# Planning the main expert slots with priority and ahead of the dual slots, turning their list in the second early slot's layer 2, and stacking the token tiles over v

## The chip, the cores and the metric

The kernel runs on one core of one Trainium2 chip. The metric is the device time of one execution in microseconds (us), and the number to compare with is the median of three runs: 804.94 us (804.16 to 805.5). TensorE (PE, with its weight loads as PEld) multiplies matrices, VectorE (DVE) and ScalarE (ACT) do elementwise work, GpSimd (POOL) issues the indirect transfers, and SyncE (SP) issues the plain ones. [...]

## The reference

Linear attention feeds a mixture of experts with one expert per token. All data are float32.

```python
# attention: 8 batches, 8 heads, 576 positions, head size 64, 128 features
proj = x @ w_phi                       # for q and for k
proj = proj - max(abs(proj))           # over the features
phi  = concat(exp(proj), exp(-proj))   # 256 features
kv, z = phi(k).T @ v, phi(k).sum(positions)
x = (phi(q) @ kv) / (phi(q) @ z + 1e-6)          # [8, 576, 512] over all heads

# experts: 8 of them, 512 -> 1024 -> 512
logits = x @ w_gate;  local = sigmoid(x @ w_local)
e[s] = argmax(logits[s]) if s == 0 or local[s] < 0.5 else e[s-1]
out[s] = softmax(logits[s])[e[s]] * (relu(x[s] @ w1[e[s]]) @ w2[e[s]])
```

There are 4,608 tokens. How many go to which expert is known only when the kernel runs.

## The kernel before, in words

**Attention** (`step` and what it calls) runs over pairs of chunks of 128 positions. `proj` multiplies k and q by `w_phi` and makes the tiles `sb` and `kp`; `qtr` turns the q part into `qp` (pool `feat`, eight buffers); `kv` adds up `kvp` from `kp` and `v`; `num` multiplies `qp` with the finished `kvs` into the PSUM tile `nm` (line 312), from which `end` (lines 329 to 340) writes the normalised rows `xo` to DRAM and keeps the gate logits `lg`. `kq` and `v` are loaded ahead into pool `front2`; `m`, `sb`, `kp` lie in `front3`.

**Gating** (`gate`) runs once for each of four batch pairs. It finds each token's expert and its place in the expert's list, and nine indirect writes on POOL (line 555) scatter token number and probability into the DRAM table `lst`. For the last pair the PE steps of this work are set between the matmuls of the first early slot, through the hooks in `soon`.

**Early slots.** Half way through attention `plan_early` picks three groups of 256 tokens (each a "slot" with two units of 128 tokens of one expert), for which the first batch pairs already give enough tokens. `slots(self.eslots)` computes these three after attention. A slot is: `tokens` (PE turns gathered rows `xg` at line 905; ACT and DVE split them into the high part `xhi` and the low part `xlo`, lines 914 and 915), `layer1` (four steps `f2` of 24 matmuls into one of two PSUM buffers `l1`; each gives `hh` on ACT, line 954, and `hl` on DVE, line 955), and `layer2` (for each unit `k` 24 matmuls into `l2`, then `y` on DVE, line 1006, and an indirect write of the rows, line 1009). Every product is three matmuls (lines 919 to 921). The weights come in eight pieces per slot: SP loads a piece into `wraw` (line 842), ACT rounds it to `whi` (line 852), DVE makes `wlo` (line 853).

**Main slots.** `plan_main` counts the tokens of all experts (`units_so_far`), subtracts what the early slots took, and hands out the rest to slots of four, two and one unit ("m" in the names of its tiles), and the rests of at most 64 tokens to dual slots, in which two experts share a tile ("h0", "h1"). It is a generator in two parts. The first part is all the planning on DVE, tiny operations on 36 by 8 numbers, and the three indirect reads of the lists from `lst` into the tile `lr` in `fetch` (line 616: the main list by `p_rim`, the duals' lists by two `p_rih`). The second part turns `lr` on PE (line 629) and copies it to `tok` and `prob`, with which the rows `xg` of the main slots are gathered. Before the change DVE plans the duals first and the main slots after them, and POOL reads the lists in the order of the program and of the planner below. SP reads the expert numbers of the main slots (`value_load`, line 829) before it can load their weights.

**Where the two parts stand.** `later` is a list of functions that the first early slot's `layer2` calls after `f` 0 and 2 of each unit; its third, after `f` 0 of unit 1, is the first part. `asides={1: more}` runs the second part between layer 1 and layer 2 of the second early slot. `final` calls the generator once more in the third early slot, when it has already ended.

**Order and memory.** Except for the PE order of attention, the order on each engine is made by a planner that walks the program with its own costs: of what is ready it takes what stands first in the program. `tc.high_priority()` moves the instructions inside it ahead of all others that are ready; `issue_after` keeps a PE instruction behind a given one. Pools are laid out as two stacks. On the right stack `open_main` puts its pools where attention's right pools were: `front2` at the end of the memory (20,088 bytes per partition: four `kq` of 3,072, then five `v` of 1,560), then `front3` (about 28,770), then `feat` (eight `qp` of 4,096). A new tile waits until the readers of every old tile that it overlaps are done. Before the change the weight pool `moe_wr` (32,768 bytes: four `whi`, four `wlo`) comes first and the token pool `moe_x2` (16,384 bytes: two `xhi`, two `xlo`) after it, so that `moe_x2` reaches from 32,768 to 49,152 bytes from the end, and its first `xhi` overlaps the last `qp` buffer by about 300 bytes. On the left stack `open_rest` puts the pool `moe_l1`, with three more `wraw` buffers, where the pool with `lr` was; the first main weight load goes there and so has to wait until `lr` is turned.

Of the kernel before, what the change touches and what calls it, by code (L numbers as in the profile page):

```python
# [9 lines left out]
I32 = mybir.dt.int32  # L10
AF = mybir.ActivationFunctionType
ALU = mybir.AluOpType
AX = mybir.AxisListType
# [4 lines left out]
DM, E, FF = 512, 8, 1024  # L18
# [4 lines left out]
NU_E = NT // 128  # L23
# [7 lines left out]
WE, WR, WL = 8, 4, 1  # L31
# [13 lines left out]
HALFWAY, EARLY, QUADS, PAIRS, SINGS, GUARD, DUALS, GUARD_D = 2, 3, 3, 7, 10, 6, 4, 2  # L45
# [4 lines left out]
class Kernel:  # L50
# [9 lines left out]
    def run(self):  # L60
        nc, tc, A = self.nc, self.tc, self.A
        act, dve = self.act, self.dve
        with ExitStack() as root:
            self.const = self.mkpool(root, "const", 1, "left")
            dram = self.mkpool(root, "dram", 1, "left", DRAM)
            self.xs = dram.tile([NT + 1, DM], F32, name="xs")


            self.lst = dram.tile([E * NT + 128, PLACE], F32, name="lst")
            first = self.const.tile([128, 256], F32, name="first")  # L70
            self.sp.dma_start(first[:, 128:256], A["first"][:, 384:512])
            self.ident, self.w2 = first[:, 0:128], first[:, 128:256]
            self.cnt = self.const.tile([128, E], BF16, name="cnt")
            dve.memset(self.cnt, 0.0)

            warm = self.const.tile([128, E], BF16, name="warm")
            act.activation(warm, self.cnt, AF.Exp)

            self.wgi = self.const.tile([128, NHP, 2, 9], F32, name="wgi")
            self.pool.memset(self.wgi, 0.0)  # L80

            self.vs = [[self.const.tile([128, 2, D + 1], F32, name=f"vs{k}{b}") for b in (0, 1)] for k in (0, 1)]
            for x in self.vs:
                for t in x:
                    self.pool.memset(t, 0.0)

            self.moe_early = self.mkpool(root, "moe_e", WE, "left")
            self.mxg = self.mkpool(root, "moe_xg", 2, "left")
            back, front = ExitStack(), ExitStack()
            self.back2 = self.mkpool(back, "back2", 2, "left")  # L90
            self.small = self.mkpool(back, "small", 1, "left")

            self.pr = self.small.tile([128, 2, NC, PLACE], F32, name="pr")
            self.pool.memset(self.pr, 0.0)
            self.pskv = self.mkpool(back, "pskv", 1, "left", PSUM)
            self.psb = self.mkpool(back, "psb", 2, "left", PSUM)


            self.front2 = self.mkpool(front, "front2", 2, "right")
            self.front3 = self.mkpool(front, "front3", 3, "right")  # L100
            self.feat = self.mkpool(front, "feat", 8, "right")
            self.psf = self.mkpool(front, "psf", 2, "right", PSUM)
            self.wphases = [(self.moe_early, WE)]

            self.scattering = False
            self.tail, self.eslots, self.scattered = False, [], []
            self.g, self.ch, self.kvb, self.lg = {}, {}, {}, {}
            n = NBP * NHP * NC
            self.todo, self.turns, self.gates, self.background = [], [], [], []
            self.fetched = 0  # L110
            for gi in range(3):
                self.fetch_kqv(gi)
                if gi == 0:
                    self.sp.dma_start(first[:, 0:128], A["first"][:, 256:384])
                    self.consts()
            with tc.manual_schedule(engines={mybir.EngineType.PE}):
                for p in range(n // 2):
                    while self.fetched < n // 3 and self.fetched * 3 < 2 * p + 8:
                        self.fetch_kqv(self.fetched)
                    if FILL <= p < FILL + 4:  # L120
                        self.fill(p - FILL)
                    self.step(p, n)
            self.tail = True
            p = n // 2
            while p < n // 2 + KVLAG + 1 or self.todo or self.turns or self.gates:
                self.step(p, n)
                p += 1
            for x in self.background:
                for _ in x:
                    pass  # L130
            front.close()
            self.open_main(root)
            plan = self.plan_main()
            more = lambda: next(plan, None)
            go = self.advance

            def rest():
                for _ in self.last_gate:
                    pass
            no = lambda: None  # L140
            self.slots(self.eslots, {1: more}, more, soon=[no, self.fetched_last, go, no, go, no, go, rest],
                       later=[no, no, more])
            back.close()
            self.open_rest(root)
            self.moe()
# [452 lines left out]
    def fetch(self, es, k, n, name, wait, halves=()):  # L598
# [8 lines left out]
        while self.scattering:  # L607
            yield STEP
        full = n
        n += DUALS if halves else 0  # L610
        lr = self.small.tile([NU + DUALS, 128 * PLACE], F32, name="lr")[0:n]
        parts = [(lr[0:full], 128, ri[0:full, :])]
        w = 64 * PLACE
# [96 lines left out]
    def plan_main(self):  # L710
        dve = self.dve
# [1 line left out]
        u1, u = self.units_so_far(127, 7, "m1"), self.units_so_far(63, 7, "m")  # L713
        r0 = self.psm([NU, E], "r0", I32)
        dve.tensor_sub(r0, u, self.taken)
        hf = self.psm([NU, E], "hf")
        dve.tensor_sub(hf, u1, u)
        full = self.floats(u, "full")
        ih = self.prefix(hf, "ih")

        q = self.psm([NU, 2], "q")
        dve.tensor_scalar(q[:, 0:1], self.slote[:, 0:1], 4.0, None, ALU.mult)
        dve.scalar_tensor_tensor(q[:, 0:1], self.slote[:, 1:2], 2.0, q[:, 0:1], ALU.mult, ALU.add)
        dve.tensor_scalar_add(q[:, 1:2], q[:, 0:1], 1.0)
        eh, rh = [], []
        for z in (0, 1):
            name = f"h{z}"
            es, _ = self.find(ih, hf, q[:, z:z + 1], name)
            oh = self.psm([NU, E], "oh" + name)
            dve.tensor_scalar(oh, self.iota8[0:NU, :], es, None, ALU.is_equal)  # L730
            dve.tensor_mul(oh, oh, full)
            k = self.psm([NU, 1], "k" + name)
            dve.tensor_reduce(k, oh, AX.X, ALU.add)
            dve.scalar_tensor_tensor(k, es, float(NU_E), k, ALU.mult, ALU.add)
            ri = self.psm([NU, 1], "ri" + name, I32)
            dve.tensor_scalar_mul(ri, k, 2.0)
            rh.append(ri)
            eh.append(self.experts(es, name))

        def level(r, shift, cap, name):  # L740
            fi = self.psm([NU, E], "fi" + name, I32)
# [11 lines left out]
        f1 = self.floats(r2, "f1")  # L753
        i1 = self.prefix(f1, "i1")

        over = self.psm([1, 2], "over")
        dve.tensor_scalar(over[:, 0:1], i1[0:1, E - 1:E], float(GUARD - SINGS), 0.0, ALU.add, ALU.max)
        dve.tensor_scalar(over[:, 1:2], ih[0:1, E - 1:E], float(2 * (GUARD_D - DUALS)), 0.0, ALU.add, ALU.max)
        self.more = self.psm([1, 1], "more", I32)
        dve.tensor_copy(self.more, over[:, 0:1])  # L760
        self.over = self.psm([1, 1], "overi", I32)
        dve.tensor_add(self.over, over[:, 0:1], over[:, 1:2])

        def mix(a, b, c, name):
            t = self.psm([NU, E], name)
            dve.tensor_scalar(t, a, mq, None, ALU.mult)
# [8 lines left out]
        dve.scalar_tensor_tensor(bef, p4, mps, self.taken, ALU.mult, ALU.add)  # L775
        dve.scalar_tensor_tensor(bef, p2, ms, bef, ALU.mult, ALU.add)
        es, j = self.find(incl, cnt, cq, "m")
        oh = self.psm([NU, E], "ohm")
        dve.tensor_scalar(oh, self.iota8[0:NU, :], es, None, ALU.is_equal)
        dve.tensor_mul(oh, oh, bef)  # L780
# [1 line left out]
        dve.tensor_reduce(k, oh, AX.X, ALU.add)  # L782
        dve.tensor_add(k, k, half)
        dve.scalar_tensor_tensor(k, j, size, k, ALU.mult, ALU.add)
        ei = self.experts(es, "m")
        f = self.fetch(es, k, NU, "m", 1, rh)
        next(f)
        yield
        try:
# [12 lines left out]


    def open_main(self, root):
        self.w_right = self.mkpool(root, "moe_wr", WR, "right")

        self.mxt = self.mkpool(root, "moe_x2", 2, "right")
        self.mx2 = self.mkpool(root, "moe_h2", 2, "right")
        self.psm4 = self.mkpool(root, "moe_ps1", 1, "right", PSUM)
        self.psl = self.mkpool(root, "moe_ps2", 2, "right", PSUM)  # L810
        self.wphases = [(self.moe_early, WE), (self.w_right, WR)]
# [203 lines left out]
            else:  # L1015
                held.append(put)

    def slots(self, order, asides={}, final=None, held=None, soon=(), later=()):
        first = order[0]
        for g in range(len(first["n"])):  # L1020
            for f in self.tokens(first, g):
# [3 lines left out]
        for i, s in enumerate(order):  # L1025
# [3 lines left out]
            last = len(s["n"]) - 1  # L1029
            for gi in range(last):  # L1030
                self.layer1(s, gi, [])
            between = self.tokens(new, 0, bool(soon) and i == 0) if new else [lambda: None, final] if final else []
            rest = self.layer1(s, last, between, () if i else soon)
            if soon and i == 0:
                rest = later
            if i in asides:
                asides[i]()
            for f in between:
                f()
            for gi in range(last + 1):  # L1040
# [140 lines left out]
```

## Time and profile before

| what | value |
|---|---|
| median of three runs | 804.94 us (804.16 to 805.5) |
| the profiled execution's own time | 804.99 us |
| its span, first to last instruction | 803.1 us |
| PE busy | 770.4 us (96%) |
| DVE busy | 513.1 us (64%) |
| ACT busy | 401.0 us (50%) |
| POOL busy | 157.3 us (20%) |
| attention's last matmul (line 312) ends | about 320.4 us |
| early slots on PE | about 321.6 to 404 us |
| main and dual slots | from there to the end |

The span and the time differ by 1.9 us, which lie before the first and after the last instruction. Of the views, "waits" adds up for one engine who it waited for; "timeline" lists instructions in order of time, with the idle time before them and its releaser in square brackets; "windows" gives, for a stretch of time, the busy time and the number of instructions of each engine, the granted clock of TensorE and the share and rate of the transfers; "lines" gives groups of instructions with busy time and mean duration. A q behind an engine's name is its sequencer, which waits and issues transfers.

### The profile page before, as it was taken

How to read it: one execution, taken by the hardware profiler on the slowest of the kernel's cores; microseconds unless marked ns; L12 is line 12 of the kernel's file. 1: busy time of each engine (PE TensorE's matmuls, PEld its weight loads, DVE VectorE, ACT ScalarE, POOL GpSimd, SP SyncE). 2: the span in 40 equal slices, each digit the busy share in tenths (PEclk: the TensorE clock that was granted, in tenths of full speed). 3: DMA queues.
4: the chain of work that ended last, by engine and by line, in shares of the span. 5: the costliest groups of instructions: out<-in, count | busy, mean ns of one | idle time of the engine just before them, and what ended most of it. 6: DMA issues, size and time to landing. Idle time of an engine off the chain costs nothing.

```text
span 803.1 us, 23175 instructions
## 1 busy us (share of the span) xinstructions
PE 770.4 (96%) x9674; PEld 678.4 (84%) x9674; DVE 513.1 (64%) x939; ACT 401.0 (50%) x708; POOL 157.3 (20%) x165
## 2 busy tenths in 40 slices
PE   6899999999998998999899999999999999999993
PEld 5899989998897888888798997698998998589983
DVE  5677798789878886785653224543866823768631
ACT  4666666666687565333542123532744713657410
POOL 0000001200275231064231202201421311111100
PEclk9999999999999999999999999999999999999997
DMA  6754545454576723455932775832966769959300
GB/s 198 220 152 127 134 133 143 129 140 126 176 227 208 232 71 96 145 170 178 362 124 93 271 268 206 294 101 94 350 219 202 272 229 411 356 193 320 124 27 14
DMA packets 77227, 151.29 MB, mean 188 GB/s; under 512 B 8524, under 2 KB 50828, under 8 KB 77078
## 3 DMA queue, kind: packets, MB, share of 16 engines
q1 hardware_dynamic: 67424, 127.33, 49.6%
q0 software_dynamic: 7424, 20.08, 7.0%
q10 hardware_dynamic: 2272, 2.37, 0.9%
q8 instruction: 77, 1.26, 0.6%
q14 instruction: 30, 0.25, 0.1%
HBM read 128.21 MB, written 22.06 MB: 187 GB/s over the span
## 4 chain that ended last, share of the span: by engine, by line
PE 83%; DVE 7%; DMA 4%; issue 2%; ACT 2%; SPq 1%; another core or an unknown queue 0%; POOLq 0%; DVEq 0%; POOL 0%; ACTq 0%
PE l L919 15%; PE l L921 15%; PE l L920 15%; PE kvp L253 8%; PE pj L211 8%; PE nm L312 8%; PE qt L231 4%; PE l L932 4%; DMA wraw<-in_w2h 2%; PE tr L905 2%; DVE m L214 1%; DVE sb L216 1%; PE nm L291 1%; DMA kq<-in_kqT 1%; DMA wraw<-in_w1h 1%
## 5 line engine op out<-in xcount | busy, mean ns | idle before, releaser
L852 ACT CAST whi<-wraw 128x1024 fp32r<-128x1024 f32 x136 | 142.2, 1048 | 165.3 <-PE l L921 67.2
L853 DVE TENSOR_TENSOR wlo<-wraw,whi 128x1024 fp32r<-128x1024 f32 x128 | 156.3, 1223 | 71.0 <-ACT whi L852 69.6
L919 PE MATMUL l<-xhi,whi 128*128 128x256 f32 x512 | 147.1, 288 | 1.4 <-ACT xhi L914 1.3
L920 PE MATMUL l<-xlo,whi 128*128 128x256 f32 x512 | 144.8, 283 | 1.3 <-DVE xlo L915 1.3
L921 PE MATMUL l<-xhi,wlo 128*128 128x256 f32 x512 | 144.7, 283 | 0.0
L919 PE MATMUL l<-whi,hh 128*128 128x512 f32 x288 | 114.8, 399 | 1.6 <-ACT hh L954 1.6
L214 DVE TENSOR_REDUCE m<-pj 128x8 f32<-128x1024 f32 x72 | 87.8, 1219 | 44.5 <-PE pj L211 44.1
L921 PE MATMUL l<-whi,hl 128*128 128x512 f32 x288 | 113.9, 396 | 1.4 <-DVE hl L955 1.4
L920 PE MATMUL l<-wlo,hh 128*128 128x512 f32 x288 | 113.1, 393 | 0.0
L234 ACT ACTIVATE qp<-qt 128x512 f32<-128x512 f32 x144 | 84.6, 604 | 53.6 <-PE qt L231 53.2
L220 ACT ACTIVATE kp<-sb 128x512 f32<-128x512 f32 x144 | 82.8, 622 | 51.2 <-DVE sb L216 43.5
L919 PEld LDWEIGHTS l<-xhi,whi 128*128 128x128 f32 x512 | 97.6, 191 | 4.3 <-issue 2.2
L920 PEld LDWEIGHTS l<-xlo,whi 128*128 128x128 f32 x512 | 97.7, 191 | 1.9 <-DVE xlo L915 1.5
L921 PEld LDWEIGHTS l<-xhi,wlo 128*128 128x128 f32 x512 | 97.8, 191 | 0.1
L211 PE MATMUL pj<-first,kq 64*128 64x128 f32 x1152 | 86.1, 291 | 6.7 <-DMA kq<-in_kqT 6.7
L216 DVE TENSOR_TENSOR sb<-pj,m 128x1024 f32<-128x1024 f32 x72 | 88.1, 1224 | 4.1
L312 PE MATMUL nm<-kvs,qp 128*64 128x74 f32 x2304 | 86.3, 228 | 1.5 <-ACT kvs L293 1.5
L1009 POOL DMA_INDIRECT out<-y,p_tokm x31 | 39.1, 1263 | 244.4 <-DVE y L1006 243.8
L211 PEld LDWEIGHTS pj<-first,kq 64*128 64x128 f32 x1152 | 72.2, 193 | 12.3 <-issue 5.0
L312 PEld LDWEIGHTS nm<-kvs,qp 128*64 128x64 f32 x2304 | 79.1, 136 | 2.2 <-ACT kvs L293 2.0
L253 PE MATMUL kvp<-v,kp 128*64 128x65 f32 x2048 | 76.2, 224 | 0.0
L955 DVE SCALAR_TENSOR_TENSOR hl<-l,hh 128x512 fp32r<-128x512 f32 x64 | 43.9, 686 | 43.5 <-ACT hh L954 43.5
(229 smaller groups left out, 1053.3 us busy)
## 6 DMA issues: line engine op xcount, KB each, us to landing
wraw<-in_w1h SPq DMA_DIRECT2D x68, 512.0 KB, 5.7
wraw<-in_w2h SPq DMA_DIRECT2D x68, 512.0 KB, 4.8
kq<-in_kqT SPq DMA_DIRECT2D x47, 384.0 KB, 3.9
v<-in_va SPq DMA_DIRECT2D x48, 195.0 KB, 3.7
xs<-xo SPq DMA_DIRECT2D x48, 128.0 KB, 2.1
whi<-in_w1h SPq DMA_DIRECT2D x8, 512.0 KB
wlo<-in_w1h SPq DMA_DIRECT2D x8, 512.0 KB, 5.5
whi<-in_w2h SPq DMA_DIRECT2D x8, 512.0 KB
```

What stands on the lines that cost most here:

```text
L211: self.last_pe = self.pe.matmul(t[:, h, i % 2, j, :], kq[r, j, s], self.w2[r], start=True, stop=True)
L214: dve.tensor_reduce(m, f, AX.X, ALU.max, apply_absolute_value=True)
L216: self.last_dve = dve.tensor_sub(sb.rearrange("p h c j f -> p (h c j) f"), f, m.unsqueeze(2).broadcast_to([128, 8, 128]))
L220: self.last_act = act.activation(kp[:, :, :, sg, :].rearrange("p c h f -> p h c f"), sb[:, :, :, 0], AF.Exp, scale=1.0 - 2 * sg)
L234: self.act.activation(qp[:, sg], t, AF.Exp, scale=1.0 - 2 * sg)
L253: self.pe.matmul(self.kvp[r, sg, h], self.ch[i]["kp"][:, h, sg, r], self.v(i, b)[:, h], start=first and n < 2, stop=last and n >= 6)
L312: self.pe.matmul(e["t"][r, c - c0, h, :], self.ch[i]["qp"][:, sg, h, q0 + r.start:q0 + r.stop], kvs[:, sg, h, :], start=sg == 0, stop=sg == 1)
L852: self.act.copy(hi, raw)
L853: (low or self.dve).tensor_sub(lo, raw, hi.bitcast(F32))
L919: mm(o, ah, bh, start=first, stop=False)
L920: mm(o, ah, bl, start=False, stop=False)
L921: self.last_pe = mm(o, al, bh, start=False, stop=last)
```

## The change

Four things change.

1. `open_main` opens the token pool `moe_x2` before the weight pool `moe_wr`. The token tiles then take the last 16,384 bytes, over the `kq` and `v` buffers, and the weight tiles 16,384 to 49,152 bytes from the end; now the first `whi` buffer overlaps the last `qp` by about 300 bytes.
2. `more` runs each part of `plan_main` inside `tc.high_priority()`.
3. In `plan_main` the planning of the duals and of the two overflow counts becomes a function `duals`, which `fetch` calls after the main list's row numbers `p_rim` are made. The main slots' operations come first in the program, and their expert numbers `ei` directly after `find`.
4. The second part of `plan_main`, with the turning of `lr`, moves from between the layers of the second early slot into its layer 2, after `f` 0 of unit 1. `asides` and `final` go, and `later` becomes a list for each slot.

No instruction of the computation is added or removed.

```diff
             plan = self.plan_main()
-            more = lambda: next(plan, None)
+            def more():
+                with tc.high_priority():
+                    next(plan, None)
...
-            self.slots(self.eslots, {1: more}, more, soon=[no, self.fetched_last, go, no, go, no, go, rest],
-                       later=[no, no, more])
+            self.slots(self.eslots, soon=[no, self.fetched_last, go, no, go, no, go, rest], later=[[no, no, more]] * 2)
...
         full = n
-        n += DUALS if halves else 0
+        if halves:
+            n, halves = n + DUALS, halves()
...
     def plan_main(self):
...
         dve.tensor_sub(r0, u, self.taken)
-        hf = self.psm([NU, E], "hf")
-        dve.tensor_sub(hf, u1, u)
-        full = self.floats(u, "full")
-        ih = self.prefix(hf, "ih")
...
         es, j = self.find(incl, cnt, cq, "m")
+        ei = self.experts(es, "m")
...
         dve.scalar_tensor_tensor(k, j, size, k, ALU.mult, ALU.add)
-        ei = self.experts(es, "m")
-        f = self.fetch(es, k, NU, "m", 1, rh)
+        hf = self.psm([NU, E], "hf")
+        eh = []
+
+        def duals():
+            dve.tensor_sub(hf, u1, u)
+            full = self.floats(u, "full")
+            ih = self.prefix(hf, "ih")
...
+            return rh
+
+        f = self.fetch(es, k, NU, "m", 1, duals)
...
     def open_main(self, root):
+        self.mxt = self.mkpool(root, "moe_x2", 2, "right")
         self.w_right = self.mkpool(root, "moe_wr", WR, "right")
-        self.mxt = self.mkpool(root, "moe_x2", 2, "right")
...
-            between = self.tokens(new, 0, bool(soon) and i == 0) if new else [lambda: None, final] if final else []
+            between = self.tokens(new, 0, bool(soon) and i == 0) if new else []
             rest = self.layer1(s, last, between, () if i else soon)
-            if soon and i == 0:
-                rest = later
-            if i in asides:
-                asides[i]()
+            if i < len(later):
+                rest = list(later[i])
```

More of the change, by code (lines that the diff above doesn't have):

```diff
@@ L715, in plan_main @@
         dve.tensor_sub(r0, u, self.taken)
-        hf = self.psm([NU, E], "hf")
-        dve.tensor_sub(hf, u1, u)
-        full = self.floats(u, "full")
-        ih = self.prefix(hf, "ih")
[L721 to L738, printed above, removed]
         def level(r, shift, cap, name):
@@ L754, in plan_main @@
         i1 = self.prefix(f1, "i1")
[L756 to L762, printed above, removed]
         def mix(a, b, c, name):
@@ L784, in plan_main @@
         dve.scalar_tensor_tensor(k, j, size, k, ALU.mult, ALU.add)
-        ei = self.experts(es, "m")
-        f = self.fetch(es, k, NU, "m", 1, rh)
+        hf = self.psm([NU, E], "hf")
[4 more added lines that the diff above has]
+            ih = self.prefix(hf, "ih")
+            q = self.psm([NU, 2], "q")
+            dve.tensor_scalar(q[:, 0:1], self.slote[:, 0:1], 4.0, None, ALU.mult)
+            dve.scalar_tensor_tensor(q[:, 0:1], self.slote[:, 1:2], 2.0, q[:, 0:1], ALU.mult, ALU.add)
+            dve.tensor_scalar_add(q[:, 1:2], q[:, 0:1], 1.0)
+            rh = []
+            for z in (0, 1):
+                name = f"h{z}"
+                es, _ = self.find(ih, hf, q[:, z:z + 1], name)
+                oh = self.psm([NU, E], "oh" + name)
+                dve.tensor_scalar(oh, self.iota8[0:NU, :], es, None, ALU.is_equal)
+                dve.tensor_mul(oh, oh, full)
+                k = self.psm([NU, 1], "k" + name)
+                dve.tensor_reduce(k, oh, AX.X, ALU.add)
+                dve.scalar_tensor_tensor(k, es, float(NU_E), k, ALU.mult, ALU.add)
+                ri = self.psm([NU, 1], "ri" + name, I32)
+                dve.tensor_scalar_mul(ri, k, 2.0)
+                rh.append(ri)
+                eh.append(self.experts(es, name))
+            over = self.psm([1, 2], "over")
+            dve.tensor_scalar(over[:, 0:1], i1[0:1, E - 1:E], float(GUARD - SINGS), 0.0, ALU.add, ALU.max)
+            dve.tensor_scalar(over[:, 1:2], ih[0:1, E - 1:E], float(2 * (GUARD_D - DUALS)), 0.0, ALU.add, ALU.max)
+            self.more = self.psm([1, 1], "more", I32)
+            dve.tensor_copy(self.more, over[:, 0:1])
+            self.over = self.psm([1, 1], "overi", I32)
+            dve.tensor_add(self.over, over[:, 0:1], over[:, 1:2])
+            return rh
+        f = self.fetch(es, k, NU, "m", 1, duals)
         next(f)
@@ L1016, in layer2, with slots @@
                 held.append(put)
-    def slots(self, order, asides={}, final=None, held=None, soon=(), later=()):
+    def slots(self, order, held=None, soon=(), later=()):
         first = order[0]
```

## The prediction

> **What bounds the kernel now.** I read the page first, then who PE waits for, then the order of time on PE, ACT and SP around those waits, and last the stretches with their granted clock. The page's span and first section:
>
> ```profile
> span 803.1 us, 23175 instructions
> ...
> PE 770.4 (96%) x9674; PEld 678.4 (84%) x9674; DVE 513.1 (64%) x939; ACT 401.0 (50%) x708; POOL 157.3 (20%) x165
> ```
>
> PE sets the end, so only its idle time and its slow clock can be won. The windows view (columns: length; busy time and count of PE, PEld, DVE, ACT, POOL; clock; transfer share; GB/s) shows where these lie near the change:
>
> ```profile
> 320.36:327.24 6.88, 4.34 (x22) 4.16 (x23) 4.42 (x20) 1.34 (x3) 0.00 (x0) 0.75 0.50 158
> 391.17:398.92 7.75, 5.51 (x20) 4.05 (x20) 6.23 (x7) 5.09 (x6) 0.48 (x1) 0.78 1.02 398
> 405.00:780.00 375.00, 374.99 (x2451) 325.54 (x2450) 197.98 (x225) 158.09 (x223) 66.82 (x56) 1.00 0.63 220
> ...
> 356.00:370.50 14.50, 13.59 (x86) 11.38 (x86) 11.71 (x37) 7.10 (x9) 4.53 (x4) 1.00 0.54 177
> ```
>
> In the main slots (405 to 780 us) PE idles 0.01 us, so what is won or lost before them passes whole to the end. There are two holes. The first, where the early slots begin, has 6.88 - 4.34 = 2.54 us of idle time, and its clock of 0.75 costs 6.88 x 0.25 = 1.72 us more: 4.26 us. The second, in the third early slot, has 7.75 - 5.51 = 2.24 us idle and 7.75 x 0.22 = 1.70 us of clock: 3.94 us. Next come 14.50 - 13.59 = 0.91 us of small waits in the second early slot.
>
> **The first hole** in order of time (PE and ACT):
>
> ```profile
> 312.25 2.24 PE L312 MATMUL nm<-kvs,qp 128*64 128x74 f32 x62
> 314.43 1.09 PE L905 MATMUL tr<-first,xg 128*128 128x128 f32 x8
> ...
> 317.57 2.79 PE L312 MATMUL nm<-kvs,qp 128*64 128x74 f32 x80 [0.29 <-ACT kvs L293]
> 321.63 0.47 PE L919 MATMUL l<-xhi,whi 128*128 128x256 f32 x2 [1.27 <-ACT xhi L914]
> 323.38 0.38 PE L920 MATMUL l<-xlo,whi 128*128 128x256 f32 x1 [1.27 <-DVE xlo L915]
> ...
> 313.07 2.95 ACT L852 CAST whi<-wraw 128x1024 fp32r<-128x1024 f32 x3
> 320.46 1.07 ACT L914 CAST xhi<-tr 128x512 fp32r<-128x512 f32 x2 [2.94 <-PE nm L312]
> ```
>
> The first slot's tokens are turned by 314.43 + 1.09 = 315.52, but ACT writes `xhi` at 320.46 and names the last `nm` matmul (317.57 + 2.79 = 320.36) as its releaser. That matmul doesn't make the data; it is the last reader of the old `qp` buffer under `xhi`. PE then has nothing until `xhi`, and again until `xlo`.
>
> *What the stacking does to it.* After the change `xhi` lies over `kq` and `xlo` over the end of `kq` and `v`. The last reader of `v`, the `kvp` matmuls, is done before the 62 `nm` matmuls that begin at 312.25. So both casts can follow the turning at 315.5; ACT sits idle for 2.94 us of the time up to 320.46. Two `xhi` take 1.07 us; two `xlo` on DVE (0.68 us each, below) then end about 318.7 to 320 between the `xo` work. PE goes from the last `nm` straight into layer 1, idle time 2.54 us won. The stretch of half clock came right behind this idle time, and I take it to go with it: 1.72 us. Term: -4.26 us, with ends 0 and -4.26.
>
> [...]
>
> *What it costs.* The first right-hand `whi` buffer now lies over the last `qp`, so one of the three casts at 313.07 moves behind 320.36. It changes places with the two `xhi` (one cast of 2.95/3 = 0.98 us against 1.07 us on ACT; one `wlo` of 1.22 against two `xlo` of 1.37 on DVE). Its data are for the second early slot. One `wraw` of three stays taken some 6 us longer. I take 0, hidden by ACT's idle time; without that cover the cast stands ahead of an `hh` and costs its 0.98.
>
> **The second hole.** PE's waits between 310 and 400 us, and ACT's order there:
>
> ```profile
> PE l L919 <- ACT hh L954: 1.6, 2, 1.1
> PE l L921 <- DVE hl L955: 1.4, 3, 0.6
> ...
> 382.79 0.59 ACT L954 ACTIVATE hh<-l 128x512 fp32r<-128x512 f32 x1
> ...
> 388.74 1.05 ACT L852 CAST whi<-wraw 128x1024 fp32r<-128x1024 f32 x1 [3.08 <-DMA wraw<-in_w2h]
> 389.70 0.59 ACT L954 ACTIVATE hh<-l 128x512 fp32r<-128x512 f32 x1
> 391.11 1.05 ACT L852 CAST whi<-wraw 128x1024 fp32r<-128x1024 f32 x1 [0.82 <-DMA wraw<-in_w2h]
> 392.39 1.05 ACT L852 CAST whi<-wraw 128x1024 fp32r<-128x1024 f32 x1 [0.24 <-DMA wraw<-in_w2h]
> 393.35 0.59 ACT L954 ACTIVATE hh<-l 128x512 fp32r<-128x512 f32 x1
> 393.84 1.04 ACT L852 CAST whi<-wraw 128x1024 fp32r<-128x1024 f32 x1
> ```
>
> PE waits for `hh` and `hl` of the third slot, and these stand in ACT's list behind casts of the first main slot's weights, which wait for transfers that run at a share of 1.02. Why do those transfers come so late? SP's waits from 361 to 378 us, its reads of the expert numbers, its loads; PE's turning of the list; POOL's reads of the list and their landing:
>
> ```profile
> SPq L842 <- DMA lr<-lst,p_rim: 3.2, 1, 3.2
> ...
> SPq L842 <- PE pt L629: 0.5, 1, 0.5
> ...
> L829 SPq TENSOR_LOAD <-p_eim x14: 266/274/562, 362.2 to 369.9; - x14
> ...
> 374.57 2.06 SPq L842 DMA_DIRECT2D wraw<-in_w1h  x4
> ...
> 371.87 0.39 PE L921 MATMUL l<-whi,hl 128*128 128x512 f32 x1
> 374.02 0.41 PE L629 MATMUL pt<-first,lr 40*128 40x40 f32 x2
> ...
> 359.03 0.91 POOL L616 DMA_INDIRECT lr<-lst,p_rih  x1 [3.21 <-DVE p_f L646]
> 360.25 1.66 POOL L616 DMA_INDIRECT lr<-lst,p_rih  x1 [0.30 <-DVE p_lem L586]
> 368.92 0.92 POOL L616 DMA_INDIRECT lr<-lst,p_rim  x1 [5.67 <-DVE p_rim L605]
> DMA to landing us min/median/max: 2.8/4.3/5.1
> ```
>
> SP spends 8 us (362.2 to about 370.2) on 14 expert numbers, then 3.7 us on `lr`: the main list is read last, at 368.92, because DVE plans it last.
>
> *Moved planning, reads and turning.* With the main chain first and all of it urgent, the three reads follow each other from about 359.0 at a pitch of 1.2 us; the last goes out near 361.5 and lands at most 5.1 us later, 366.6. The expert numbers come sooner too, so SP's 8 us fall among the third slot's loads, where they push weights that layer 2 wants only after the `hh` above; hidden, and 0. What holds `lr` now is its new place on PE. After `f` 0 of unit 1 means after the matmul at 371.87, so at about 372.1 instead of 374.02: 1.9 us earlier on PE's own clock. The whole of it shifts with the first term, and the landing at 366.6 is still ahead of 372.1 - 4.3 = 367.8; were the reads later than that, the 1.9 would shrink. The main `xg` reads on POOL come 1.9 us earlier with `tok`.
>
> *What 1.9 us earlier loads bring.* ACT's order is written out beforehand. Now two casts stand between the third and the fourth `hh`. The planner places casts by its own transfer times; with loads 1.9 us earlier it has room for one more cast ahead of each `hh`. The third `hh` then follows the cast of 391.11 instead of 388.74: 391.11 + 1.05 - 1.9 = 390.26, later than 389.70. The fourth follows the cast of 393.84: 393.84 + 1.04 - 1.9 = 392.98, earlier than 393.35 by 0.37. The last wait decides: -0.37, the clock still falls. If the order stays as it is, the term is -1.9 and the clock's -1.70, -3.60. I take -0.37, because the same planner that set casts ahead of `hh` before has the same cause to do it again.
>
> *DVE's burst of planning.* DVE rows of 346.2 to 368.7 us, and the first `hl` of the second slot:
>
> ```profile
> 346.20:368.70 22.50, 21.80 (x142) 19.10 (x141) 20.85 (x89) 12.28 (x15) 11.40 (x10) 1.00 0.56 168
> ...
> L853 DVE TENSOR_TENSOR wlo<-wraw,whi 128x1024 fp32r<-128x1024 f32 x9 | 11.0, 1219 | 0.6 <-ACT whi L852 0.5
> L955 DVE SCALAR_TENSOR_TENSOR hl<-l,hh 128x512 fp32r<-128x512 f32 x4 | 2.7, 674 | 0.0
> L915 DVE TENSOR_TENSOR xlo<-tr,xhi 128x512 fp32r<-128x512 f32 x2 | 1.4, 684 | 1.0 <-ACT xhi L914 1.0
> L1006 DVE TENSOR_SCALAR y<-l,p_probe 128x512 f32<-128x512 f32 x1 | 0.7, 732 | 0.0
> ...
> 346.20:356.10 9.90, 4.87 (x4) 0.00 (x0) 1.00 0.48 126
> 356.08 0.67 DVE L955 SCALAR_TENSOR_TENSOR hl<-l,hh 128x512 fp32r<-128x512 f32 x1
> ```
>
> Planning is 20.85 - 11.0 - 2.7 - 1.4 - 0.7 = 5.05 us of DVE. Ahead of `hl` at 356.08 stand four `wlo` (4.87) and one `y` (0.73), so up to 9.9 - 4.87 - 0.73 = 4.3 of it is there already. Made urgent, at most 0.75 us more gets ahead of `hl` and of `y`, which PE awaits; against that, the 0.91 us of small waits behind it can shrink as the planning is gone. Ends +0.75 and -0.91; I take 0, between them. The swap of main and dual planning has the same operations.
>
> **Sum** against the execution's own 804.99 us (median of the runs 804.94, so no correction): 804.99 - 4.26 - 0.37 = 800.36 us.
>
> **Rivals.**
>
> *Both holes close* (0.23): ACT's order stays and the loads' 1.9 us count whole. For it: 1.9 of 2.24 us idle would do. Against it: the same lists are planned anew. 804.99 - 4.26 - 3.60 = 797.13.
>
> *The gap closes, the slow clock stays* (0.07): The half clock comes from something that stays, such as the short waits among the `nm` matmuls before 320 us. 804.99 - 2.54 - 0.37 = 802.08. Against it stands that in both holes half clock follows idle time at once. [...]
>
> *The change doesn't open the start* (0.14): `xhi` is written late for another reason, such as the `wlo` and `xo` work on DVE holding `xlo` beyond the last `nm`, so that PE waits as long. For it: `xlo` has its own 1.27 us wait. Against it: the releaser in the row is PE's `nm`, not DVE. 804.99 - 0.37 = 804.62.
>
> *Slower: ACT's list is filled with casts* (0.18). With the main slots planned sooner, the planner may set not one but many casts ahead of the third slot's `hh`. Transfers are at their limit there, so the `hh` wait for real landings. If all eight casts stand ahead of the second `hh`, it ends its wait at 392.98 instead of 382.79, 10.2 us later; the two `l1` buffers are full by then, so PE loses that, less the 2.24 it loses now: +8.0. 804.99 - 4.26 + 8.0 = 808.7. With seven casts (392.39 + 1.05 - 1.9 = 391.54) it is +6.5 and 807.2, with six (390.26) +5.2 and 805.9. So it becomes slower from the seventh cast ahead of the second `hh`; against it, 1.9 us is room for one.
>
> **How the numbers follow.** The forecast has 0.38. A measurement of this kernel can't tell less than 0.2%, 1.6 us, from no change. Faster: forecast, both holes and gap alone, 0.38 + 0.23 + 0.07 = 0.68. Same: 0.14. Slower: 0.18. The range reaches below 797.13 by the 0.91 of small waits, to 796.2, rounded to 796.0, and above 804.62 by the 0.75 of planning and part of the six-cast case, to 806.0; it leaves out the slower rival.
>
> **What would show it.** Right: `xhi` released before the last `nm`, no PE idle between `nm` and layer 1, granted clock 1.00 there; the main list read before the duals' by POOL; `lr` turned about 1.9 us sooner after unit 1 begins; a `whi` cast right after the last `nm`; the second hole still there with one more cast ahead of each late `hh`. Wrong: PE waiting for `xlo` at the start; a new wait for `y` or `hl` in the second slot; idle time of several us behind `hh` in the third.

## The result, and the profile after

The kernel after takes 799.53 us (median of 11 runs, 796.47 to 801.45) against 804.16 us (median of 11 runs, 802.04 to 806.61) for the kernel before: a ratio of 0.9941, 95% interval 0.9929 to 0.9953, so 4.63 us faster. The profiled execution took 796.47 us, the lowest of its runs, so the two profiles differ by 8.52 us, more than the medians do. The page of after begins:

```profile
span 794.5 us, 23170 instructions
...
PE 764.4 (96%) x9674; PEld 674.0 (85%) x9674; DVE 512.9 (65%) x939; ACT 401.7 (51%) x708; POOL 158.3 (20%) x165
```

The windows view of after (columns as before: length; busy time and count of PE, PEld, DVE, ACT, POOL; clock; transfer share; GB/s) for the start of the early slots, the second slot, the third slot and the main slots:

```profile
318.12:325.00 6.88, 6.88 (x58) 6.73 (x58) 6.42 (x19) 4.89 (x6) 2.78 (x2) 1.00 0.60 149
346.20:366.20 20.00, 18.34 (x124) 16.30 (x124) 16.15 (x24) 9.45 (x12) 10.25 (x9) 1.00 0.62 202
377.50:391.00 13.50, 11.32 (x66) 9.35 (x65) 10.50 (x12) 7.97 (x11) 0.97 (x1) 1.00 1.01 394
397.00:772.00 375.00, 374.99 (x2452) 325.40 (x2452) 197.40 (x225) 158.00 (x223) 67.57 (x56) 1.00 0.62 219
```

The first hole is gone: in the 6.88 us behind the last `nm` matmul PE is busy all the time, at full clock. In the second slot the idle time is now 20.00 - 18.34 = 1.66 us. The third slot still waits: 13.50 - 11.32 = 2.18 us, 2.24 before; but its clock is 1.00 now, 0.78 before. The main slots are as full as before, so all that is won ahead of them reaches the end. PE's and ACT's order of time at the start (line numbers are up to nine higher than before: 314 was 312, 914 was 905, 923 was 914, 928 to 930 were 919 to 921, 861 was 852, 963 was 954):

```profile
313.53 0.41 PE L281 MATMUL nm<-first,kf 128*128 128x128 f32 x2 [0.19 <-DVE rc L331]
...
315.33 2.79 PE L314 MATMUL nm<-kvs,qp 128*64 128x74 f32 x80
318.05 0.39 PE L928 MATMUL l<-xhi,whi 128*128 128x256 f32 x1
318.27 0.28 PE L929 MATMUL l<-xlo,whi 128*128 128x256 f32 x1
...
314.41 0.58 ACT L923 CAST xhi<-tr 128x512 fp32r<-128x512 f32 x1
...
315.49 0.58 ACT L923 CAST xhi<-tr 128x512 fp32r<-128x512 f32 x1 [0.40 <-PE tr L914]
318.22 2.94 ACT L861 CAST whi<-wraw 128x1024 fp32r<-128x1024 f32 x3 [2.14 <-PE nm L314]
321.18 0.60 ACT L963 ACTIVATE hh<-l 128x512 fp32r<-128x512 f32 x1
```

`xhi` now follows the turning and layer 1 follows `nm` without a gap. Three `whi` casts, not one, wait for the last `nm` in their turn, and `hh` comes right behind them. The short waits among the last `nm` matmuls shrank too. In the trace of before PE has

```profile
315.99 0.41 PE L279 MATMUL nm<-first,kf 128*128 128x128 f32 x2 [0.47 <-DVE rc L329]
316.86 0.41 PE L291 MATMUL nm<-wgi,ks 128*64 128x18 f32 x8 [0.46 <-ACT ks L282]
```

and the 0.29 us at 317.57 that the prediction shows, 1.22 us together; after, 0.19 us is left.

Second slot, turning and the reads of the lists (PE with one cast and its `wlo`, then POOL and SP of after, each in order of time):

```profile
350.74 0.47 PE L928 MATMUL l<-whi,hh 128*128 128x512 f32 x1 [0.89 <-DVE p_rim L607]
...
361.67 1.05 ACT L861 CAST whi<-wraw 128x1024 fp32r<-128x1024 f32 x1 [0.67 <-DMA wraw<-in_w2h]
...
362.75 1.22 DVE L862 TENSOR_TENSOR wlo<-wraw,whi 128x1024 fp32r<-128x1024 f32 x1 [0.49 <-ACT whi L861]
363.90 0.74 DVE L1015 TENSOR_SCALAR y<-l,p_probe 128x512 f32<-128x512 f32 x1
...
364.70 0.50 PE L928 MATMUL l<-whi,hh 128*128 128x512 f32 x1 [0.77 <-DVE y L1015]
...
365.27 0.39 PE L930 MATMUL l<-whi,hl 128*128 128x512 f32 x1
365.59 0.41 PE L632 MATMUL pt<-first,lr 40*128 40x40 f32 x2
...
356.05 0.92 POOL L619 DMA_INDIRECT lr<-lst,p_rih  x1 [4.05 <-DVE wlo L862]
...
359.85 1.45 POOL L619 DMA_INDIRECT lr<-lst,p_rim  x1 [0.31 <-issue]
...
366.13 2.04 SPq L851 DMA_DIRECT2D wraw<-in_w1h  x4
```

PE waits twice. The 0.89 us stand behind DVE's planning, whose last operation `p_rim` is done at 350.65. The 0.77 us don't: the planning is over by then, and `y` stands in DVE's list behind a `wlo`, whose cast waits 0.67 us for a weight load. POOL still reads the main list last, though its row numbers are there before 350.74. And `lr` is turned right after the first three matmuls of unit 1. In the third slot ACT now has two casts ahead of each `hh` (one pair is shown, then PE's longest wait):

```profile
379.00 1.05 ACT L861 CAST whi<-wraw 128x1024 fp32r<-128x1024 f32 x1 [0.73 <-DMA wraw<-in_w2h]
381.39 1.05 ACT L861 CAST whi<-wraw 128x1024 fp32r<-128x1024 f32 x1 [1.34 <-DMA wraw<-in_w2h]
382.34 0.59 ACT L963 ACTIVATE hh<-l 128x512 fp32r<-128x512 f32 x1
...
379.69 0.39 PE L928 MATMUL l<-xhi,whi 128*128 128x256 f32 x1 [1.43 <-DVE hl L964]
```

PE's waits there are no longer for an `hh`. The longest, 1.43 us, is for the `hl` of the second step, which stands on DVE behind the `wlo` of such a cast; 0.45 us for another `hl` and 0.29 us for a `y` follow, several microseconds apart.

Everything below ran on three chips on which the kernel before took 816.02, 816.91 and 814.85 us (medians of 23 to 29 runs) and not 804; so ratios of the experiments are compared with each other on one chip, and the last group asks what is different there.

### The profile page after: what moved, and what is told of

It is laid out like the page before. It is cut to its first block, busy times and chain, and to the rows that moved or that the text cites. A ratio compares the mean times of both kernels' runs of the same rounds, so it can differ in the third digit from the quotient of the medians.

```text
span 794.5 us, 23170 instructions
## 1 busy us (share of the span) xinstructions
PE 764.4 (96%) x9674; PEld 674.0 (85%) x9674; DVE 512.9 (65%) x939; ACT 401.7 (51%) x708; POOL 158.3 (20%) x165
## 4 chain that ended last, share of the span: by engine, by line
PE 56%; DVE 4%; DMA 3%; issue 3%; ACT 1%; POOL 1%; another core or an unknown queue 0%; POOLq 0%; SPq 0%; DVEq 0%
PE l L928 15%; PE l L930 15%; PE l L929 15%; PE l L941 4%; DMA wraw<-in_w1h 2%; PE tr L914 2%; PE nm L314 2%; PE kvp L255 1%; DMA wraw<-in_w2h 1%; PE pj L213 1%; DVE m L216 1%; PE tr L980 1%; DVE sb L218 1%; PE qt L233 1%; ACT whi L861 1%
## 5 line engine op out<-in xcount | busy, mean ns | idle before, releaser
L213 PEld LDWEIGHTS pj<-first,kq 64*128 64x128 f32 x1152 | 71.1, 190 | 11.9 <-issue 4.9
```

Of the source, the lines that this page charges most:

```text
L213: self.last_pe = self.pe.matmul(t[:, h, i % 2, j, :], kq[r, j, s], self.w2[r], start=True, stop=True)
```

## The experiments

**Theory and rivals.** The theory: stacking the token tiles over `v` opens the start and brings the gain; planning and turning are worth about nothing. Rivals: the planning part brings it, or takes something; the third slot is where a larger gain is lost.

**The stacking alone** (the kernel before, with one edit), on the first chip:

```diff
     def open_main(self, root):
+        self.mxt = self.mkpool(root, "moe_x2", 2, "right")
         self.w_right = self.mkpool(root, "moe_wr", WR, "right")
-        self.mxt = self.mkpool(root, "moe_x2", 2, "right")
```

> The kernel before with only the token pool opened ahead of the weight pool; planning, list reads and the turning of the list as before. Theory (the stacking carries the gain): the wait for xhi and xlo and the half clock behind it at the start of the early slots go (4.3 us), and the short waits among the last nm matmuls shrink (1.1 us); the third slot's waits stay: 804.2 - 5.4 = 798.8 us, at least 4 us faster than before. Rival (planning with priority carries half): about 801.9 us.

Measured: 807.05 us, ratio 0.9894 (0.9875 to 0.9913; 4 runs). **The planning alone** (the kernel after, with these two lines in their old order), on the same chip:

> The kernel after with the two pools in the old order: only the planning with priority, main before duals, and the new place of the turning. Theory: the start keeps its hole; the waits in the second slot grow by 0.75 us and the third slot's shrink by little, so 804.2 us plus or minus 1. Rival (planning carries half): about 801.9 us.

Measured: 817.92 us, ratio 1.0021 (1.0007 to 1.0034; 12 runs). The 6.88 us behind the last `nm`, first with the stacking alone, then with the planning alone (windows):

```profile
325.49:332.37 6.88, 6.88 (x57) 6.73 (x58) 6.42 (x18) 5.05 (x6) 2.77 (x2) 1.00 0.55 150
```

```profile
328.97:335.85 6.88, 4.33 (x22) 4.16 (x23) 4.43 (x20) 1.34 (x3) 0.00 (x0) 0.75 0.45 142
```

The stacking closes the hole and the planning leaves it as it was, 2.55 us of idle time and a clock of 0.75. On this chip the stacking carries the whole gain, and some 4 us more than the first term (816.02 - 807.05 = 8.97 us, and 8.15 us on the second chip, against 4.26). About 1 us of this is expected among the last `nm` matmuls. Most of the rest seems to lie in the planning. The stacking alone has there

```profile
351.00:378.00 27.00, 25.52 (x159) 21.73 (x158) 18.72 (x63) 9.96 (x13) 13.78 (x14) 1.00 0.58 169
```

1.48 us of idle time at full clock, and 3.17 us at full clock on the second chip; the kernel before loses 6.1 us there on the third chip (below). That kernel's trace was not taken on the first two chips, so this is not shown on one chip.

**The turning put back** between the layers of the second slot, still with priority:

```diff
-            self.slots(..., later=[[no, no, more]] * 2)
+            self.slots(..., later=[[no, no, more]], asides={1: more})
...
```

> The kernel after, with the second part of the plan (the turning of the list) back between the two layers of the second early slot, still with priority. Theory: the turning now stands so early in PE's list that PE waits for the list's landing, and the planner sets four casts instead of two ahead of the third slot's first hh; 2 to 6 us slower than the kernel after, 801.5 to 805.5 us. Rival (the place of the turning doesn't matter): 799.5 us.

Measured: 817.11 us, ratio 1.0015 (0.9999 to 1.003; 10 runs). PE's waits from 345 to 420 us:

```profile
...
PE l L928 <- ACT hh L963: 2.4, 1, 2.4
...
```

The turning came at 376.43 us, seven microseconds earlier than in the kernel after on the second chip (383.54), yet `hh` of the third slot kept PE waiting 2.4 us: six casts of the main slot now stood ahead of its first `hh`, where four were expected. An earlier turning doesn't shorten this wait; the order fills with casts. What it costs in all against the kernel after can't be said on this chip, where that kernel was not run; beside its ratio on the next chip (0.9985) it is 0.003 more, or 2.4 us.

**The casts held back**: the first main slot's casts are bound behind the third slot's `hh` and `hl`.

```diff
...
+                    ia, iv = self.steps[8 + after]
+                    with self.tc.issue_after(ia), self.tc.issue_after(iv):
+                        self.split(s)
...
```

> The kernel after, with the eight casts of the first main slot's weights bound behind the third early slot's hh and hl: one before the first hh, then two, one, one and three, in place of two before each. Theory (the casts' place on ACT makes the second hole): the idle time of 2.2 us in the third slot falls below 0.6 us and the clock stays full there; 797.0 us, about 2.5 us faster than the kernel after. Rival (the transfers set it): PE waits as long, only later, for the main slot's weights or tokens; 799.5 us or more.

Measured: 815.95 us, ratio 1.0004 (0.9989 to 1.0019; 12 runs). PE's waits in the same stretch:

```profile
...
PE l L935 <- DVE y L1024: 2.9, 1, 2.9
...
```

No `hh` or `hl` is waited for any more, but the delayed work stands ahead of `y`, and PE waits 2.9 us there. The third slot's hole is not the fault of the order alone; it moves. How much of it the loads themselves would leave was not separated.

**The same four on a second chip**, now with the kernel after itself, since on the first chip every kernel with the urgent planning had come out even:

> The kernel after, unchanged, beside the others. In the study's first job the kernel before took 816 us, and PE and DVE stood still for some microseconds at 287 to 291 us and 351 to 363 us with no releaser. Theory (these stalls belong to that chip, and the change's gain is the start of the early slots): with the stalls absent, 0.994 of before, as first measured. Rival (the stalls come and go with the kernel's order): another ratio than 0.994 again.

> The kernel before with only the token pool opened ahead of the weight pool, again. Theory (the stacking carries the gain): 0.993 to 0.995 of before, the same as the kernel after within 1.2 us. Rival (the planning carries half): 0.997.

> The kernel after with the two pools in the old order, again: planning with priority, main before duals, the turning later. Theory: 1.000 of before, plus or minus 0.0015. Rival: 0.997.

> The kernel after with the first main slot's casts bound behind the third early slot's hh and hl, again. Theory: no wait for hh in the third slot and no fall of the clock there, 2.5 us faster than the kernel after, 0.991 of before. Rival: PE waits elsewhere as long, 0.994.

Measured: after 816.00 us, ratio 0.9985 (0.9971 to 0.9999); stacking alone 808.76, 0.9893 (0.9878 to 0.9908; 4 runs); planning alone 817.48, 1.0005 (0.9991 to 1.0018); casts held back 817.62, 1.0004 (0.9987 to 1.0021). So stacking alone is worth about 1.1% on both chips, and on these chips the planning part takes nearly all of it back, which it didn't do in the first measurement. The expectations of 0.994 for the kernel after and 0.991 with the casts held back failed. The parts don't add up: planning alone costs 0.2 and 0.05% against the kernel before, but 0.9% on top of the stacking.

**What takes it back: priority or order?** On a third chip, the kernels before and after, and the kernel after without the priority:

```diff
             def more():
-                with tc.high_priority():
-                    next(plan, None)
+                next(plan, None)
```

> The kernel before, unchanged, for its trace on this chip. Where it takes about 816 us, as beside the other runs, and not 805: theory (two stretches are slower there, whatever the change: one at 286 to 291 us, in which every engine pauses, and one in the planning): the first of them is there, with 2 to 3 us of PE idle time behind which nothing is shown and 3 to 7 us at half clock, and the planning, which is not urgent here, costs at most 2 us of such pauses. Rival (the planning pauses as long when it isn't urgent): 5 us or more of PE waits between 350 and 370 us here too.

> The kernel after, unchanged, beside the next run on one chip. Where the kernel before takes about 816 us: ratio 0.996 to 1.001, with PE waits of 3 to 5 us for p_rim behind the urgent planning. Where it takes about 805 us: ratio 0.992 to 0.996, and no such wait.

> The kernel after without the priority: the stacking, the main list's planning ahead of the duals' and the turning in the second slot's layer 2 stay, but the planner's instructions take their ordinary places among the casts' and the slots' work. Where the kernel before takes about 816 us: theory (the urgent burst of small DVE instructions costs what the stacking wins): no PE wait over 2 us for p_rim, and 807 to 811 us, ratio 0.988 to 0.993. Rival (not the urgency but the order of the lists or the early turning costs it): 814 to 818 us, ratio 0.997 to 1.002. Where the kernel before takes about 805 us, theory: within 0.3% of the kernel after; rival: over 0.3% off it.

Measured: before 814.85 us (its profiled execution 813.63), after 814.61, ratio 0.9991 (0.9972 to 1.001); without the priority 809.36, ratio 0.9923 (0.9894 to 0.9953; 6 runs). The windows of the planning, each over 25 us, before, after, and after without the priority:

```profile
355.00:380.00 25.00, 21.64 (x129) 19.33 (x129) 18.33 (x63) 10.31 (x13) 8.07 (x9) 0.86 0.50 150
362.40:369.23 6.83, 5.38 (x20) 4.51 (x20) 4.85 (x13) 3.18 (x5) 2.16 (x2) 0.50 0.90 270
```

```profile
355.00:380.00 25.00, 17.36 (x96) 16.03 (x95) 14.87 (x47) 7.70 (x11) 6.88 (x8) 0.73 0.51 162
360.30:373.95 13.65, 8.46 (x37) 8.12 (x37) 10.26 (x33) 4.77 (x7) 3.50 (x4) 0.50 0.53 170
```

```profile
355.00:380.00 25.00, 20.77 (x128) 18.13 (x127) 17.04 (x43) 9.34 (x12) 10.89 (x11) 0.93 0.46 148
361.98:365.39 3.41, 3.19 (x13) 3.03 (x14) 1.93 (x5) 0.60 (x1) 2.50 (x4) 0.50 0.89 229
```

The second line of each pair is the part at half clock. There matmuls of 128x256 follow each other at 0.21 us, at full clock at 0.12 us (before, at 366.5 and 359 us). As an estimate, half of the busy time at half clock is added to the idle time of the whole: 3.36 + 5.38 / 2 = 6.1 us before, 7.64 + 8.46 / 2 = 11.9 us after, and 4.23 + 3.19 / 2 = 5.8 us without the priority. In the first measurement the planning cost 0.9 us before and 1.66 us after, at full clock. PE's waits there (before, after, without priority; "issue" means that the profile shows nothing that was waited for):

```profile
PE l L919 <- issue: 1.3, 2, 0.8
PE l L921 <- issue: 1.1, 1, 1.1
PE l L920 <- issue: 0.9, 2, 0.5
```

```profile
PE l L928 <- DVE p_rim L607: 3.9, 1, 3.9
...
```

```profile
PE l L927 <- DVE p_rim L606: 3.0, 1, 3.0
PE l L927 <- ACT hh L962: 0.6, 1, 0.6
...
```

And DVE's order of time in the kernel after on this chip, out of its burst of planning:

```profile
353.62 0.16 DVE L577 TENSOR_TENSOR p_pl<-p_f,p_i 36x8 f32<-36x8 f32 x1 [1.11 <-DVE p_cm L739]
...
359.30 0.17 DVE L649 CAST p_f<-p_r 36x8 f32<-36x8 int32 x1 [1.10 <-DVE p_bef L748]
```

Operations of 0.16 us have pauses of 1.1 us between them, and the operation named as releaser had long been done. With the priority everything that PE awaits from DVE stands behind this burst; without it no DVE pause of over 0.3 us without a shown cause is left in the planning. So the priority is what costs here: dropping it brings 0.9991 to 0.9923, in the range that the theory gave. The planning then costs about what it costs in the kernel before (5.8 against 6.1 us). Stacking alone had 0.9893 on the other chips, so the order of the lists or the early turning may cost some more; the intervals overlap, and no run shows it. Two of the theory's details fell. A wait for `p_rim` of 3.0 us stayed without the priority, where at most 2 was expected. And the kernel before, whose planning isn't urgent, pauses as well, 3.36 us where at most 2 was expected (under the rival's 5), while the stacking alone, not urgent either, has no such pause on DVE on the first chip. The priority makes these pauses dearer; it is not the only thing that brings them, and why the stacking alone was spared is open.

The accounting of this chip's profiles: after against before wins 2.54 us in the start hole, 1.23 - 0.19 = 1.04 us among the last `nm`, 0.9 us in the third slot, and loses 11.9 - 6.1 = 5.8 us in the planning. It is also 0.99 us behind when the 62 `nm` matmuls begin, with nothing changed up to there. That is 2.3 us slower; the two profiled executions (816.50 and 813.63 us) differ by 2.9.

**Which tile over `qp`?** In the kernel before, `xlo` is allocated ahead of `xhi`, so that `xlo` has the 256 bytes of overlap with the last `qp`:

```diff
-... self.mxt.tile([128, 4, 256], F32R, name=n) for n in ("xhi", "xlo")]
+... self.mxt.tile([128, 4, 256], F32R, name=n) for n in ("xlo", "xhi")][::-1]
```

> The kernel before with one swap: xlo is allocated ahead of xhi, so that xlo and not xhi lies over the end of qp. Nothing else is moved. Theory (the first hole is the wait of xhi's cast for the last nm matmul): xhi is cast at about 315 us, 1 us behind the turning, PE goes from the last nm into l<-xhi,whi with under 0.2 us of idle time, and waits then for xlo for 0.3 to 0.9 us instead of 1.27 + 1.27; 3 to 5 us faster than before, ratio 0.993 to 0.997. Rival (ACT's and DVE's own order holds the casts back, not the overlap): both waits stay over 1 us, ratio 0.999 to 1.001.

Measured: 816.14 us, ratio 1.0002 (0.9979 to 1.0024; 10 runs). PE and ACT in order of time:

```profile
325.99 0.47 PE L919 MATMUL l<-xhi,whi 128*128 128x256 f32 x2 [1.27 <-ACT xhi L914]
327.74 0.39 PE L920 MATMUL l<-xlo,whi 128*128 128x256 f32 x1 [1.28 <-DVE xlo L915]
...
324.82 1.07 ACT L914 CAST xhi<-tr 128x512 fp32r<-128x512 f32 x2 [2.94 <-PE nm L312]
```

Nothing changed: `xhi`, which no longer touches `qp`, waits for the last `nm` as before. In the built program the swap did move the tiles, and the wait for that matmul is written in front of the cast. The program of the kernel before shows besides that the `qp` buffer under `xhi` has its last reader well ahead of the last `nm` matmul, which reads another `qp` buffer. So the wait doesn't belong to the tile that has the shared bytes; the pool as a whole has it, and a new tile can wait for readers of an old pool that it doesn't touch. The theory's place was right (moving the pool closes the hole) and its grain was wrong.

## Why the prediction was right

The median was 799.53 us against a forecast of 800.36, 0.83 us off, and the likeliest case is the one that came. The main mechanism held; that the number came so near is in part luck, as the steps show.

- *The first hole, -4.26.* Confirmed in the profile of after (idle time 2.54 to 0, clock 0.75 to 1.00), and by the stacking alone, which closes it, and the planning alone, which doesn't. Of the term, 2.54 us of idle time went in every stacked run. The 1.72 us of clock is less certain than the prediction had it: it took the half clock to come with the gap, and runs below show the same gap without it. What decides between the two was not shown; that this share of the term counted in the profile of before was luck. And the reading that the last `nm` matmul is the last reader of the `qp` buffer under `xhi` was wrong: it reads another buffer, and the pool waits for it.
- *The cost of `whi` behind the last `nm`, 0.* The cost held, the count failed: "one of the three casts moves" was three. All three follow the one wait for `nm`, 2.94 us of casts from 318.22 to 321.16, and `hh` starts at 321.18: the cover just sufficed.
- *Not in the sum: the waits among the last `nm`.* The three casts and their `wlo` left the stretch in which PE had waited for `rc`, `ks` and `kvs`. Worth 1.22 - 0.19 = 1.03 us, from the profile alone. The step that failed is the exchange of the casts with `xhi`, which was costed on ACT and DVE only for what comes after.
- *Planning, 0 between +0.75 and -0.91.* The second slot came out at 1.66 - 0.91 = +0.75 us, the upper end, but not for the reason given. Behind the burst stands one wait of 0.89 us, a little over the bound of 0.75; the small waits of before are gone, as the lower end had it; and 0.77 us are new, for a `y` behind a `wlo` whose weights were still being loaded, a term the prediction doesn't have. The bound itself was a bound for DVE as it ran in that trace; with the pauses of the third chip the planning cost 5.8 us more than before.
- *The reads of the lists.* "The main list read before the duals'" was wrong: POOL's order kept the duals ahead, with 3.8 us between the first dual read and the main one. It had no price: the main read still went out at 359.85, and PE has no gap ahead of the turning at 365.59, though its weight load waited 0.36 us for `lr` to land.
- *Turning and loads, 1.9 us earlier.* Right: `lr` turned at 365.59 behind the first matmuls of unit 1 and the first main load at 366.13, 8.44 us earlier than 374.57. The third matmul of unit 1 had itself moved by 371.87 - 365.27 = 6.60 us, so 1.84 us of it is the turning's own.
- *The third slot, -0.37.* Right that the hole stays, with one more cast ahead of each `hh`; 0.3 us too large, since the waits went from 2.24 to 2.18 us, so -0.06. The place was wrong: the last wait, for the fourth `hh`, was to decide, and PE waits most for the `hl` of the second step. And "the clock still falls" was wrong for this execution, in which the waits lie apart and the clock stays at 1.00.

With the measured sizes the steps give 804.99 - 4.26 - 1.03 + 0.75 - 0.06 = 800.4 us, near the median; what was missed cancels. The profiled execution lies 3.9 us below that. Its third slot has no half clock (1.71 us); its last `nm` ends 2.24 us earlier, of which 1.2 us are not the shorter waits and lie where nothing was changed; and 1.0 us is not accounted for.

Of the rivals, "both holes close" fell: the third slot's waits stayed. "The gap closes, the slow clock stays" fell for this hole. "The change doesn't open the start" fell with the stacking alone. The slower rival, a list filled with casts, had its mechanism seen in one experiment, with the turning between the layers (six casts ahead of the first `hh`, 2.4 us of waiting), but not in the kernel after.

## What to carry to other kernels

Where a releaser in a row makes none of the data, look for a pool that lies underneath, and move the whole pool, since swapping tiles inside it did nothing. A burst of small operations made urgent is paid by every result that PE awaits from the same engine, and its bound holds only while the engine keeps its pace: here the planning cost +0.75 us in one measurement and +5.8 us in another. Time each part of a change alone, and don't expect the parts to add up: on a chip where the whole change had 0.9985, its stacking alone had 0.9893 and was the fastest kernel tried.

## What the runs showed of the hardware that was not expected

**The same gap, with and without half clock.** Behind the last `nm`, the kernel before on the third chip:

```profile
326.79:333.67 6.88, 4.34 (x32) 4.01 (x33) 4.65 (x22) 2.31 (x5) 0.11 (x1) 1.00 0.53 154
```

These are the same two waits of 1.27 us and the same 2.5 us of idle time as in the prediction's trace, where the clock is 0.75. With `xlo` first it is 0.78; the planning alone has 0.75 on one chip and, on another, 1.00. So the clock fell behind gaps of 1.27 us in three of these five executions (0.75, 0.78, 0.75) and stayed at 1.00 in two.

In the windows of the planning above the half clock is 3.41, 6.83 and 13.65 us long: 1, 2 and 4 times 3.41 us. In the prediction's trace two of 3.41 us begin at 323.83 and 395.51, 71.68 = 21 x 3.413 us apart. Here are the 3.41 us with the waits and the next, first in that trace, then in the kernel before on the third chip, where the second ends 30.72 = 9 x 3.413 us ahead of the half clock at 362.40:

```profile
320.42:323.83 3.41, 0.93 (x5) 0.75 (x6) 3.34 (x14) 1.07 (x2) 0.00 (x0) 1.00 0.94 298
323.83:327.24 3.41, 3.41 (x19) 3.41 (x18) 1.02 (x8) 0.26 (x1) 0.00 (x0) 0.50 0.06 16
```

```profile
324.85:328.27 3.42, 2.14 (x64) 2.02 (x58) 2.52 (x11) 1.07 (x2) 0.00 (x0) 1.00 1.02 295
328.27:331.68 3.41, 2.14 (x18) 1.94 (x17) 3.02 (x14) 0.26 (x1) 0.00 (x0) 1.00 0.62 205
```

In the first trace one of these lengths holds both waits, is idle for 3.41 - 0.93 = 2.48 us, and the next has half clock. In the second the waits lie in two of them, idle for 1.28 and 1.27 us, and the clock stays at 1.00. The second half clock of the prediction's trace:

```profile
392.10:395.51 3.41, 1.70 (x7) 0.78 (x6) 3.26 (x4) 2.53 (x4) 0.00 (x0) 1.00 1.02 405
395.51:398.92 3.41, 3.41 (x13) 2.92 (x14) 2.49 (x3) 1.63 (x2) 0.48 (x1) 0.50 1.00 384
```

There the 3.41 us ahead of it are idle for 3.41 - 1.70 = 1.71 us, in waits of 1.09 and 0.62 us. The length of one gap doesn't tell in these traces: the clock fell behind these, and stayed behind 1.28 us on the third chip and 1.43 us in the third slot of the kernel after. At the places shown the idle time in 3.41 us was 2.48 and 1.71 us ahead of half clock, and at most 1.28 us where the clock stayed. No run moved the waits by themselves, so what sets the clock was not shown.

**Pauses of all engines that no view explains.** From 286 to 300 us, with nothing changed there, the kernel before in the first measurement and on the third chip:

```profile
286.00:300.00 14.00, 13.41 (x284) 11.93 (x281) 11.82 (x41) 9.19 (x20) 5.89 (x10) 1.00 0.15 43
```

```profile
286.00:300.00 14.00, 11.76 (x193) 9.80 (x192) 7.17 (x24) 5.28 (x11) 4.30 (x6) 0.88 0.13 35
```

PE is idle 1.65 us more and loses 14 x 0.12 = 1.7 us of clock. That is too low a measure: it also gets through 193 matmuls in place of 284, which by the pace of the first line is an estimated 14 x 91 / 284 = 4.5 us. Up to the end of the last `nm` matmul the two executions are 326.79 - 320.36 = 6.43 us apart, so most of it lies here. Behind that only some 2 us more come, of the 8.6 us by which they differ in all (813.63 - 804.99): the planning loses 6.1 - 0.9 = 5.2 us more on the third chip, but the start has no half clock there, 1.7 us, and about 1.4 us is not placed. Both stretches have POOL's indirect writes of the lists beside many small instructions, but so has the planning with the stacking alone, which on the first chip hardly pauses (1.48 us of idle time in 27 us). Transfers are not at a limit in the first (share 0.13). Neither was varied by itself, so the cause stays open.
